# Rewriting the prologue of an induced attention block that feeds a gated feed-forward layer

## The chip, the cores and the metric

The kernel runs on one core of one Trainium2 chip. The metric is device time in microseconds (us) of one execution, lower is better, given as a median over runs. A profile is one execution taken by the hardware profiler; its span runs from the first to the last instruction and is a little shorter than the time. The engines are PE (matrix multiply, with its weight loads listed apart as PEld), DVE (vector), ACT (activation functions), POOL (GpSimd) and SP, which here only issues DMAs. POOL also issues DMAs. Each engine executes its own instructions in the order in which the program gives them.

## What is computed

Cut to what matters, with B = 4 batches of N = 12416 rows of C = 128 columns, m = 32 inducing rows, d_ff = 1536:

```python
def _attn_ref(x, inducing):
    scale = 1.0 / np.sqrt(C)
    I = np.broadcast_to(inducing[None], (B, m, C))
    def mab(q, kv):
        s = scale * (q @ kv.transpose(0, 2, 1))
        s = s - s.max(-1, keepdims=True)
        a = np.exp(s)
        a /= a.sum(-1, keepdims=True) + 1e-09
        return a @ kv
    h = mab(I, x)          # 32 rows per batch
    return mab(x, h)

def _moe_ref(x, w_gate, w_val, w_out):
    gate = 1.0 / (1.0 + np.exp(-(x @ w_gate)))
    return gate * (x @ w_val) @ w_out
```

All inputs and the output are float32; the kernel works in float16 with float32 sums.

## The kernel before

A batch of 12416 rows is 97 chunks of 128 rows. Chunks are taken in groups of 16 (`GC`): six full groups, numbered 0 to 5 (`NG` is 6), and a seventh of a single chunk, number `NG`. `groups` (before, the single chunk is chunk 96, the last one) gives the first chunk and the length of each group. `xn[b]` holds a batch of x with rows in partitions, `xT[b]` the same turned, so that columns lie in partitions.

The work of a batch has these parts.

- **Loads.** `x_load` (L76) issues one DMA on POOL's queue per group, which also casts to float16. All loads of batch 0, then the three weights `wg16`, `wv16`, `wo16` (L116 to L118), then all of batch 1 are issued at the start (L91 to L120). Later batches are loaded from within the main loop.
- **Stage 1**, the softmax over all 12416 rows for each of the 32 inducing rows. For a group: `x_turn` (L446) turns 16 chunks on PE and copies them out of PSUM, 8 by DVE (L453) and 8 by ACT (L454); `s1_score` gives scores (PE, L162) and their negated maximum `nm1` (DVE, L169); `s1_exp` (ACT, L181) gives exponentials and their sums `l1`; `s1_turn_pe` turns them on PE (L194) with a DVE copy (L196); `s1_sum` multiplies them with x (PE, L210) and ACT copies the result to `hst` (L217). The groups thus have a maximum of their own each.
- **Combine** (`combine`, from L250). The groups' maxima are brought to one: a DVE minimum over groups, a float32 matmul to bring 128 values into one row (L255), a minimum over the four partition groups (L257), a copy that spreads it (L261), a matmul back into a column (L266), a copy (L270). Then the groups' weights `w1` (ACT, L273), the weighted sums (L276 to L298), two float32 matmuls (L304, L305), the division (L307 to L311) that gives `hT`, and `hw`, which is h times the gate and value weights (L326 to L336). In batch 0 (`fast`) the weighted sum over groups is on DVE (L279, L284), in later batches on POOL.
- **Stage 2**, the softmax of each row over the 32 inducing rows: scores (L346), maximum (L357), which is split into two bfloat16 parts on POOL (L361, L363) and added on PE (L370), exponential (L379), sum, reciprocal (L405), the product spread to four copies (L407), and a turn by a DMA of SP's queue (`s2_turn_dma`, L417). The first four chunks (`BC`) of batch 0 are turned on PE instead (L485, L489).
- **Main loop.** A block of four chunks has 12 slices of d_ff in 8 steps. A step multiplies `a2` by `hw` for gate and value (PE, L535), takes tanh of the gate (ACT, L551), forms (t + 1) times the value (DVE, L560), and adds the product with `wo16` (PE, L590). A finished block is scaled by ACT (L597), turned by a DMA of SP (L599) and stored by a DMA of POOL (L608).

For batch 0, loads, stage 1, combine and the first group's stage 2 stand ahead of the main loop: this is the prologue. It is an order written out by hand (L459 to L492). Its loop transposes group i+2, scores group i+1, turns the exponentials of group i and sums group i-1 in one turn. Everything for the later batches is placed within the main loop by `beside`, by slots of two steps: `loads` and `work` hold the slot at which each begins; stage 1 of batch 1 begins at slot 5, and the DMA transposes of its x (`x_transpose_dma`, L85, on SP's queue) at slot 0.

PSUM is used up: the tags `g1`, `v1`, `m`, `acc` have one bank each, `g2` and `v2` two.

Of the kernel before, what the change touches and what calls it, by code (L numbers as in the profile page):

```python
# [16 lines left out]
P = 128  # L17
GC = 16
# [7 lines left out]
def kernel(  # L26
# [21 lines left out]
    groups = [(s * GC, GC) for s in range(NG)] + [(NG * GC, NLO)]  # L48
# [23 lines left out]
    def x_load(b, s):  # L72
        c0, n = groups[s]
        if b not in xn:
            xn[b] = xnp.tile([P, NCH, C], F16, tag="xn", name=f"xn_{b}")
        nc.gpsimd.dma_start(xn[b][:, c0 : c0 + n, :], xv[b, :, c0 : c0 + n, :])  # L76
# [37 lines left out]
    x_load(0, 5)  # L114
    x_load(0, 6)
    nc.gpsimd.dma_start(wg16[:], moe_w_gate.rearrange("c (i t f) -> c i t f", t=2, f=P))  # L116
    nc.gpsimd.dma_start(wv16[:], moe_w_val.rearrange("c (i t f) -> c i t f", t=2, f=P))
    nc.gpsimd.dma_start(wo16[:], moe_w_out.rearrange("(j p) c -> p j c", p=P))  # L118
    for g in range(len(groups)):
        x_load(1, g)  # L120
# [9 lines left out]
    one1 = const.tile([1, 1], F32, tag="one1")  # L130
    nc.vector.memset(one1[:], 1.0)
# [72 lines left out]
    def s1_sum(b, s, a1, tag):  # L204
# [12 lines left out]
        nc.scalar.copy(out=hsts[b % 2][0:R, s, :], in_=hp[0:R, :])  # L217
        summed[b] += 1

# [24 lines left out]
    def combine(b, fast):  # L244
        q = b % 2
        nm1, l1, hst = nm1s[q], l1s[q], hsts[q]
        while summed[b] < NS:
            yield
        mn = bp.tile([P, 1], F32, tag="mn")
        nc.vector.tensor_reduce(out=mn[:], in_=nm1[:], axis=AX.X, op=ALU.min)  # L250
        yield
        yield
        yield "take"
        row_ps = ps.tile([1, P], F32, tag="m", name="row_ps")
        nc.tensor.matmul(row_ps[:], mn[:], identf[:], start=True, stop=True)  # L255
        row = bp.tile([1, m], F32, tag="row")
        nc.vector.tensor_reduce(  # L257
            out=row[:], in_=row_ps[:].rearrange("o (g k) -> o k g", g=4), axis=AX.X, op=ALU.min
        )
        row4 = bp.tile([1, 4, m], F32, tag="row4")  # L260
        nc.vector.tensor_copy(out=row4[:], in_=row[:].unsqueeze(1).to_broadcast((1, 4, m)))  # L261
        yield "give"
        yield
        yield "take"
        col_ps = ps.tile([P, 1], F32, tag="m", name="col_ps")
        nc.tensor.matmul(  # L266
            col_ps[:], row4[:].rearrange("o g k -> o (g k)"), one1[:], start=True, stop=True
        )
        col = bp.tile([P, 1], F32, tag="col")
        nc.vector.tensor_copy(out=col[:], in_=col_ps[:])  # L270
        yield "give"
        w1 = bp.tile([P, NS], F32, tag="w1")
        nc.scalar.activation(out=w1[:], in_=nm1[:], func=AF.Exp, bias=col[:], scale=-1.0)  # L273
        yield
        lw = bp.tile([P, NS], F32, tag="lw")
        nc.vector.tensor_mul(out=lw[:], in0=l1[:], in1=w1[:])  # L276
        eng = nc.vector if fast else nc.gpsimd
        hx = bp.tile([P, NS, C], F32, tag="hx", bufs=1)
        eng.tensor_tensor(  # L279
            out=hx[:], in0=hst[:], in1=w1[:].unsqueeze(2).to_broadcast((P, NS, C)), op=ALU.mult  # L280
        )
        if fast:
            hsum = bp.tile([P, C], F32, tag="hsum")
            nc.vector.reduce_sum(out=hsum[:], in_=hx[:].rearrange("p s c -> p c s"), axis=AX.X)  # L284
            hsum = hsum[:]
        else:
            k = NS
            while k > 1:
                r = k // 2
# [28 lines left out]
        for hf in range(2):  # L318
            if not fast:
                yield "take"  # L320
# [16 lines left out]
            if not fast:  # L337
                yield "give"
# [391 lines left out]
```

## Time and profile before

| | |
|---|---|
| time, median of 3 runs | 794.26 us (793.11 to 795.95) |
| time of the profiled execution | 795.01 us |
| its span | 793.1 us |
| busy: PE, DVE, ACT, POOL | 670.7, 745.4, 672.8, 238.2 us |
| first matmul of the main loop | 38.75 us |
| first DVE product of the main loop (L560) | 40.45 us |
| last DVE product ends | 783.2 us |
| mean granted clock of PE | 0.967 |

Busy time is summed over the instructions of an engine. The three engines that compute are each busy for most of the span, DVE for 94% of it. A line of the timeline has the start in us, the length in us, the engine, the source line, the operation, written and read tiles, the shape, how many instructions are merged in it, and in brackets how long the engine was idle ahead of it and what ended that.

### The profile page before, as it was taken

Reading aid. Unit: us, or ns where it says so; the run is one execution under the profiler, and the core shown is the slowest. Engines: PE = TensorE matmul, PEld = TensorE weight load, DVE = VectorE, ACT = ScalarE, POOL = GpSimd, SP = SyncE. Lnnn points to the kernel's source line nnn. Section 1 sums busy time; section 2 is a strip of 40 time slices with the busy share of each in tenths; the row PEclk is TensorE's granted clock in tenths of the full one; section 3 lists DMA queues with packets and bytes.
Section 4 is the critical chain, followed back from the end, with each engine's and each line's share of the span. In section 5 each row is a group of like instructions: output and inputs, shape, how many; then the busy total and the mean of one; then the engine's idle time right before and its main releaser. Section 6 shows DMA issues by size and latency. Waiting matters only on the chain.

```text
span 793.1 us, 13966 instructions
## 1 busy us (share of the span) xinstructions
PE 670.7 (85%) x4729; PEld 230.8 (29%) x4729; DVE 745.4 (94%) x948; ACT 672.8 (85%) x1001; POOL 238.2 (30%) x396
## 2 busy tenths in 40 slices
PE   6588889888888888888888888988888888888884
PEld 4222223222232222322222222322323222223221
DVE  4689999999999999999998999999999999999994
ACT  4389989888989999878988898988898898899993
POOL 4131341532331422444404123143233133133200
PEclk9679999999999999989999999999999999999997
DMA  9958654536439566355338754241431431441421
GB/s 178 204 108 168 120 111 84 103 77 116 87 75 198 95 102 138 81 98 100 64 80 163 131 93 91 57 81 47 83 86 43 90 87 28 100 87 40 103 60 46
DMA packets 171015, 77.44 MB, mean 98 GB/s; under 512 B 154784, under 2 KB 155328, under 8 KB 170944
## 3 DMA queue, kind: packets, MB, share of 16 engines
q1 hardware_dynamic: 150672, 37.23, 28.8%
q0 software_dynamic: 20272, 39.33, 21.0%
q8 instruction: 37, 0.61, 0.3%
q14 instruction: 34, 0.28, 0.1%
HBM read 27.80 MB, written 25.43 MB: 67 GB/s over the span
## 4 chain that ended last, share of the span: by engine, by line
DVE 42%; PE 24%; issue 21%; ACT 10%; DMA 2%; POOL 0%; POOLq 0%; ACTq 0%; DVEq 0%
DVE u L560 37%; PE acc_ps L590 11%; PE v_ps L535 9%; ACT t L551 8%; DMA xn<-in_x_dram 2%; DVE nmx L357 2%; PE s_ps L370 1%; DVE nm L169 1%; PE g_ps L535 1%; ACT a1T L181 1%; ACT o L597 1%; DVE rs L405 1%; DVE hwt L336 0%; PE hp_ps L210 0%; PE s_ps L346 0%
## 5 line engine op out<-in xcount | busy, mean ns | idle before, releaser
L560 DVE SCALAR_TENSOR_TENSOR u<-t,v_ps 128x1024 f16<-128x1024 f16 (+1 forms) x776 | 693.1, 947 | 19.0 <-PE g_ps L535 7.3
L551 ACT ACTIVATE t<-g_ps 128x1024 f16<-128x1024 f32 (+1 forms) x776 | 598.8, 817 | 81.5 <-PE g_ps L535 67.0
L535 PE MATMUL v_ps<-a2r,hwt 32*128 32x512 f16 (+1 forms) x1188 | 294.7, 374 | 94.8 <-DVE u L560 87.6
L590 PE MATMUL acc_ps<-u,wo 128*128 128x512 f16 (+1 forms) x1200 | 325.2, 383 | 1.4 <-ACT o L597 0.7
L535 PE MATMUL g_ps<-a2r,hwt 32*128 32x512 f16 (+1 forms) x1188 | 297.4, 381 | 0.8 <-ACT t L551 0.6
L535 PEld LDWEIGHTS <-hwt 32*128 32x128 f16 x2400 | 102.8, 91 | 355.0 <-issue 346.7
L590 PEld LDWEIGHTS <-wo 128*128 128x128 f16 x1200 | 86.1, 98 | 145.3 <-issue 99.3
L407 POOL TENSOR_TENSOR a2n<-e,rs 128x2048 f16<-128x2048 f16 (+2 forms) x28 | 87.3, 3119 | 82.2 <-DVE rs L405 73.7
L608 POOL DMA_DIRECT2D out_dram<-on x100 | 57.0, 570 | 143.8 <-DMA on<-o 134.1
L597 ACT ACTIVATE o<-acc_ps 128x512 f16<-128x512 f32 (+1 forms) x100 | 59.2, 592 | 9.5 <-PE acc_ps L590 7.1
L361 POOL CAST hi<-nmx 128x16 bf16<-128x16 f32 (+3 forms) x29 | 5.7, 195 | 203.1 <-DVE nmx L357 203.0
L387 POOL TENSOR_TENSOR sum<-e 128x256 f32<-128x256 f16 (+1 forms) x27 | 16.0, 591 | 70.2 <-ACT e L379 70.2
L387 POOL TENSOR_TENSOR sum<-sum 128x128 f32<-128x128 f32 (+3 forms) x108 | 31.3, 290 | 8.5
L76 POOL DMA_DIRECT2D xn<-in_x_dram x28 | 15.4, 557 | 11.1 <-DMA xn<-in_x_dram 7.2
L346 PE MATMUL s_ps<-hT,xT 128*128 128x32 f16 x388 | 18.2, 180 | 0.6
L181 ACT ACTIVATE a1T<-s_ps,nm 128x512 f16<-128x512 f32 (+1 forms) x28 | 17.9, 639 | 0.4 <-DVE nm L169 0.4
L169 DVE TENSOR_REDUCE nm<-s_ps 128x1 f32<-128x512 f32 (+1 forms) x28 | 17.3, 618 | 0.5 <-PE s_ps L162 0.5
L346 PEld LDWEIGHTS <-xT 128*128 128x128 f16 x388 | 13.5, 97 | 13.4 <-issue 13.1
L357 DVE TENSOR_REDUCE nmx<-s_ps 128x16 f32<-128x512 f32 (+3 forms) x29 | 17.3, 596 | 0.0
L379 ACT ACTIVATE e<-s_ps 128x512 f16<-128x512 f32 (+3 forms) x29 | 15.2, 524 | 1.5 <-PE s_ps L370 1.5
L454 ACT COPY xT<-xt_ps 128x1024 f16<-128x1024 f16 x6 | 6.1, 1012 | 10.8 <-DVE xT L453 10.8
L453 DVE COPY xT<-xt_ps 128x1024 f16<-128x1024 f16 x6 | 4.1, 692 | 9.6 <-PE xt_ps L451 9.6
(78 smaller groups left out, 182.1 us busy)
## 6 DMA issues: line engine op xcount, KB each, us to landing
out_dram<-on POOLq DMA_DIRECT2D x96, 256.0 KB, 2.6
xn<-in_x_dram POOLq DMA_DIRECT2D x24, 512.0 KB, 8.5
on<-o SPq DMA_TRANSPOSE x100, 2.4
a2r<-a2n SPq DMA_TRANSPOSE x28, 6.0
wg<-in_moe_w_gate_dram POOLq DMA_DIRECT2D x1, 384.0 KB, 16.4
wv<-in_moe_w_val_dram POOLq DMA_DIRECT2D x1, 384.0 KB, 16.5
wo<-in_moe_w_out_dram POOLq DMA_DIRECT2D x1, 384.0 KB, 16.2
xT<-xn SPq DMA_TRANSPOSE x21, 4.7
```

The costliest lines, as they stand in the source:

```text
L169: nc.vector.tensor_reduce(out=nm1s[b % 2][0:R, s : s + 1], in_=s1[0:R, 0 : w * P], axis=AX.X, op=ALU.max, negate=True,)
L181: nc.scalar.activation(out=a1T[0:R, 0 : w * P], in_=s1[0:R, 0 : w * P], func=AF.Exp, bias=nm1s[b % 2][0:R, s : s + 1], accum_out=l1s[b % 2 ...
L346: nc.tensor.matmul(s2[:, j, :], xT[b][:, c + j, :], hT16[b][:], start=(j == 0), stop=False, skip_group_check=True,)
L357: nc.vector.tensor_reduce(out=nmx[:, 0:n], in_=s2[:, 0:n, :], axis=AX.X, op=ALU.max, negate=True)
L387: nc.gpsimd.tensor_tensor(out=d[:, 0:n, :], in0=src[:, :, 0:w], in1=src[:, :, w : 2 * w], op=ALU.add)
L407: eng.tensor_tensor(out=a2n[:, 0:n, :, :], in0=e[:, 0:n, :].unsqueeze(2).to_broadcast((P, n, 4, m)), in1=rs[:, 0:n].unsqueeze(2).unsqueeze ...
L535: nc.tensor.matmul(pt[:, k, col : col + W], hw[st["b"]][r : r + 32, j // 2, :], a2r[r : r + 32, o : o + nb, :].rearrange("p j t -> p (j t) ...
L551: nc.scalar.activation(out=st["t"][:, :, 0:w], in_=st["g"][:, :, 0:w], func=AF.Tanh, scale=0.5)
L560: nc.vector.scalar_tensor_tensor(out=st["u"][:, :, 0:w], in0=st["t"][:, :, 0:w], scalar=1.0, in1=st["v"][:, :, 0:w], op0=ALU.add, op1=ALU. ...
L590: nc.tensor.matmul(acc[:, 0:W], wo16[:, j, :], st["u"][:, k, col : col + W], start=first, stop=last)
L597: nc.scalar.mul(out=o16[:, 0:W], in_=acc[:, 0:W], mul=0.5)
L608: nc.gpsimd.dma_start(ov[st["b"], :, c : c + nb, :], on[:, 0:nb, :])
```

## The change

- The single chunk is now chunk 0 and the groups start at chunk 1. `x_load` of group 0 takes chunk 0 along (17 chunks, one DMA), and group 5 of batch 0 is loaded by two DMAs of 12 and 4 chunks. No load of x of the single chunk is left.
- Ahead of the prologue only x of batch 0 is loaded. `wg16` and `wv16` are issued on POOL behind the maximum of group 4, `wo16` and the first two loads of batch 1 behind the first group's stage 2 maximum, the other loads of batch 1 from within the main loop (slots 0, 3, 6, 9).
- The order of stage 1 in the prologue is a new one, shown below: the single chunk right behind group 0, then per group transposes, the turn of the group before, scores, exponentials, the sum of the group before. ACT now takes the first 8 chunks of `x_turn` and DVE the other 8, and neither waits for the other. The scores of group 4 stand ahead of group 5's transposes, its exponential behind them.
- The groups 0 to 2 and the single chunk get a common maximum of their own and are combined on POOL while groups 3 to 5 run. The weights of what is left are worked out from the maxima alone, by `s1_weights`, with copies from one group of 32 partitions to another in place of the two matmuls. The last group's sum is read from PSUM.
- `combine`, which is now for batches 1 to 3 only, uses `s1_weights` with all its copies and reductions on DVE.
- In the first stage 2, the maximum of the first four chunks is subtracted on DVE and doesn't go over POOL and PE; both copies of `hw` are on ACT; the remaining 12 chunks are spread as 4 on DVE and 8 on POOL, with a DMA transpose each.

The diff, cut to its core:

```diff
-    groups = [(s * GC, GC) for s in range(NG)] + [(NG * GC, NLO)]
+    groups = [(NLO + s * GC, GC) for s in range(NG)] + [(0, NLO)]
...
-    x_load(0, 5)
-    x_load(0, 6)
-    nc.gpsimd.dma_start(wg16[:], ...)
-    nc.gpsimd.dma_start(wv16[:], ...)
-    nc.gpsimd.dma_start(wo16[:], ...)
-    for g in range(len(groups)):
-        x_load(1, g)
+    x_load(0, 5, 12)
...
+    def s1_weights(nm1, eng):
+        n = nm1.shape[1]
+        quad = bp.tile([m, 4, n], F32, tag=f"quad{n}", name="quad")
+        for g in range(4):
+            eng.tensor_copy(out=quad[:, g, :], in_=nm1[32 * g : 32 * g + 32, :])
+        col = bp.tile([P, 1], F32, tag="col")
+        for g in range(4):
+            nc.vector.tensor_reduce(out=col[32 * g : 32 * g + 32, :],
+                in_=quad[:].rearrange("k g s -> k (g s)"), axis=AX.X, op=ALU.min)
+        w1 = bp.tile([P, n], F32, tag=f"w{n}", name="w1")
+        nc.scalar.activation(out=w1[:], in_=nm1, func=AF.Exp, bias=col[:], scale=-1.0)
+        return w1
+    def add_tree(eng, x, k):
+        while k > 1:
+            r = k // 2
+            eng.tensor_tensor(out=x[:, 0:r], in0=x[:, 0:r], in1=x[:, k - r : k], op=ALU.add)
+            k -= r
...
         if n == GC:
-            nc.vector.tensor_copy(out=xT[b][:, c0 : c0 + 8, :], in_=xt[:, 0, :, :])
-            nc.scalar.copy(out=xT[b][:, c0 + 8 : c0 + 16, :], in_=xt[:, 1, :, :])
+            one = nc.scalar.copy(out=xT[b][:, c0 : c0 + 8, :], in_=xt[:, 0, :, :])
+            for j0, j1 in ((8, cut), (cut, GC)) if cut else ((8, GC),):
+                two = nc.vector.tensor_copy(
+                    out=xT[b][:, c0 + j0 : c0 + j1, :], in_=xt[:, 1, j0 - 8 : j1 - 8, :])
+                tc.declare_no_dep(two.ins, one.ins, reason="each reads a bank of its own")
...
     x_turn(0, 0, "g2")
-    for i in range(-1, NS + 2):
-        if 0 <= i + 2 < NS:
-            x_turn(0, i + 2, ("g2", "v2")[i % 2])
-        if 0 <= i + 1 < NS:
-            aT_of[i + 1] = s1_exp(0, i + 1, s1_score(0, i + 1, ("g1", "v1")[(i + 1) % 2]))
-        if 0 <= i < NS:
-            a1_of[i] = s1_turn_pe(0, i, aT_of[i])
-        if 0 <= i - 1 < NS:
-            s1_sum(0, i - 1, a1_of[i - 1], "acc")
-    for _ in combine(0, True):
-        pass
+    x_turn(0, NG, "v2")
+    exp(0, score(0))
+    exp(NG, s1_score(0, NG, "v1"))
+    turn(NG)
+    total(NG)
+    last = NG - 1
+    for i in range(1, last):
+        x_turn(0, i, ("g2", "v2")[i % 2])
+        turn(i - 1)
+        s1 = score(i)
+        if i < last - 1:
+            exp(i, s1)
+        total(i - 1)
+        if i == early:
...
+            for k, s in enumerate(list(range(early)) + [NG]):
+                nc.gpsimd.tensor_scalar_mul(
+                    out=hx[:, k, :], in0=hst[:, s, :], scalar1=wf[:, k : k + 1])
+            hpart = add_tree(nc.gpsimd, hx, 1 + early)
+    x_turn(0, last, ("g2", "v2")[last % 2], 12)
+    exp(last - 1, s1)
+    exp(last, score(last))
+    nc.gpsimd.tensor_copy(out=nmf[:, 1:late], in_=nm1[:, early:last])
+    nc.gpsimd.dma_start(wg16[:], ...)
+    nc.gpsimd.dma_start(wv16[:], ...)
+    nc.gpsimd.tensor_copy(out=nmf[:, late:], in_=nm1[:, last:NG])
+    turn(last - 1)
+    total(last - 1)
+    w1 = s1_weights(nmf[:], nc.gpsimd)
+    turn(last)
+    hp = total(last, "g1", True)
...
+    nc.vector.tensor_scalar_mul(out=hsum[:], in0=hpart, scalar1=w1[:, 0:1])
+    for k in range(1, 1 + late):
+        nc.vector.scalar_tensor_tensor(out=hsum[:],
+            in0=hp[:] if k == late else hst[:, early + k - 1, :],
+            scalar=w1[:, k : k + 1], in1=hsum[:], op0=ALU.mult, op1=ALU.add)
...
+    s2_score(0, NLO, 0, BC, s2_a, True)
...
+    nc.vector.tensor_tensor(out=low[:], in0=s2_a[:, 0:BC, :],
+        in1=nmx_a[:].unsqueeze(2).to_broadcast((P, BC, m)), op=ALU.add)
...
+    hw_a = hw_fill(0, 0, "g1")
+    s2_score(0, NLO + BC, 0, GC - BC, s2_b)
     hl_b = s2_max(GC - BC, s2_b)
+    nc.gpsimd.dma_start(wo16[:], ...)
+    x_load(1, 0)
+    x_load(1, 1)
+    hw_b = hw_fill(0, 1, "v1")
...
+        if b == 0:
+            for g in range(2, NG):
+                loads.append((3 * (g - 2), "x", 1, g))
```

Here `score`, `exp`, `turn` and `total` are `s1_score`, `s1_exp`, `s1_turn_pe` and `s1_sum` for batch 0; `early` is 3 and `late` is 3; `hw_fill` issues the four matmuls of one half of `hw`.

## The prediction

> **What bounds the kernel now.** I read the page first. It puts 94% busy on DVE, and its costliest group is the gated product of the main loop:
>
> ```profile
> L560 DVE SCALAR_TENSOR_TENSOR u<-t,v_ps 128x1024 f16<-128x1024 f16 (+1 forms) x776 | 693.1, 947 | 19.0 <-PE g_ps L535 7.3
> ```
>
> So 693.1 of the 793.1 us of the span are one DVE instruction, repeated 776 times, with 19.0 us of idle time before it. The change leaves these 776 alone. What it can move is the stretch before the first of them, and whatever it adds to DVE between them. I therefore read the timeline of the first 45 us next (columns: start, length, engine, line, operation, tiles, count, and the idle time before it):
>
> ```profile
> 6.75 1.89 PE L451 MATMUL xt_ps<-ident,xn 128*128 128x128 f16 x16 [3.67 <-DMA xn<-in_x_dram]
> 8.68 0.69 DVE L453 COPY xT<-xt_ps 128x1024 f16<-128x1024 f16 x1 [4.95 <-PE xt_ps L451]
> 9.21 1.89 PE L451 MATMUL xt_ps<-ident,xn 128*128 128x128 f16 x16 [0.57 <-DMA xn<-in_x_dram]
> 9.40 1.01 ACT L454 COPY xT<-xt_ps 128x1024 f16<-128x1024 f16 x1 [7.40 <-DVE xT L453]
> 11.02 0.62 PE L162 MATMUL s_ps<-xT,indT 128*32 128x512 f16 x4
> 11.74 0.68 DVE L169 TENSOR_REDUCE nm<-s_ps 128x1 f32<-128x512 f32 x1
> 12.76 0.69 ACT L181 ACTIVATE a1T<-s_ps,nm 128x512 f16<-128x512 f32 x1
> 13.34 0.20 ACT L181 ACTIVATION_READ_ACCUMULATOR a1T<-s_ps,nm 128x1 f32 x1
> ...
> 19.05 1.07 PE L451 MATMUL xt_ps<-ident,xn 128*128 128x128 f16 x16 [0.28 <-DMA xn<-in_x_dram]
> ...
> 29.80 1.66 DVE L284 TENSOR_REDUCE hsum<-hx 128x128 f32<-128x896 f32 x1
> ...
> 38.75 0.61 PE L535 MATMUL g_ps<-a2first,hwt 32*128 32x512 f16 x2 [0.60 <-DVE a2first L489]
> ...
> 40.45 1.22 DVE L560 SCALAR_TENSOR_TENSOR u<-t,v_ps 128x1024 f16<-128x1024 f16 x1 [1.75 <-ACT t L551]
> ```
>
> Three things are to be seen. Loads of x land every 2.43 us (6.75, 9.2, 11.6 and so on to 19.05) and the PE transposes follow them: stage 1 of batch 0 keeps step with the loads. It can, because `x_turn` runs two groups ahead of the exponentials. From the last full group (19.05) to the first gate matmul (38.75) there pass 19.70 us, a chain with one instruction at a time. And the same 16 transposes take 1.89 us at first and 1.07 us later: PE starts at half its clock. It changes at 14.3 us, after 7.5 us of nearly unbroken work. After 24.8 it is at half again, and in the loop it works without a gap from 41.0 and is granted the full clock only at 48.7:
>
> ```profile
> 47.00:48.00 1.00, 1.00 (x6) 0.22 (x6) 0.53 (x1) 0.19 (x1) 0.00 (x0) 0.50 1.19 229
> 48.00:49.00 1.00, 1.00 (x4) 0.12 (x3) 0.93 (x1) 0.96 (x2) 0.00 (x0) 0.66 1.18 218
> 49.00:50.00 1.00, 1.00 (x9) 0.32 (x8) 0.98 (x2) 1.00 (x3) 0.37 (x1) 1.00 0.57 107
> ```
>
> (Busy time of PE, weight loads, DVE, ACT and POOL by microsecond; the third number from the end is the granted clock. Before 24 us this column shows 1.00 even where the transposes take 1.89, so there the durations speak.)
>
> **The change, part by part, against the profiled execution** (span 793.10, time 795.01, so 1.91 outside the span; the median is 794.26, 0.75 lower). I follow the first gate matmul, now at 38.75. Each hand-over between engines costs 0.05 in these rows.
>
> *Start of stage 1.* The first load has 17 chunks, 0.15 us more: transposes at 6.90 to 8.79. The two xT copies now run side by side, so the score waits for ACT's 1.01 alone (9.85) and not for 0.69 + 1.01: a gain of 0.7. Score 0.62, maximum 0.68, exponential 0.58: 11.85. Now the single chunk (group NG) is put ahead of group 1 on PE, and its exponential (0.35 + 0.18), transpose (0.18), copy (0.17) and sum (0.26) must follow group 0's on each engine. PE executes in order, so x_turn of group 1, whose data lie there at 9.35, starts at 13.0 and not 9.2. This costs 3.8.
>
> *The loop over groups 1 to 4.* The look-ahead is gone: ACT's queue reads copy(i), exp(i), hst(i-1), copy(i+1), and exp(i) needs the score that needs copy(i). At full clock one turn is copy 1.01, score 0.40, maximum 0.68, exponential until the next may start 0.58 + 0.10, hst 0.17, with hand-overs 3.09 us. At half clock PE closes the circle: transposes 1.89, copy 1.01, score 0.55, sum 0.50, hand-overs 0.10: 4.05 us. Both are longer than the 2.43 of the loads. The last group's transposes start at 13.04 + 4 x 4.05 = 29.2 at half clock, against 19.05 now: +10.2. At full clock after the first turn they start at 26.2: +7.1. That weights and the second batch's x are taken out of the queue ahead gains nothing here, since x was first in that queue already.
>
> *The last group to the gate.* The maxima are combined from nm alone, beside the sums: a POOL copy and four shifted copies (0.2 each, the nearest row is the 0.19 cast of 128x4, starts 0.12 apart), four DVE reductions (0.15 each by the 128x7 one), exponential 0.30. The two fp32 matmuls with their copies (25.2 to 28.2), the 1.08 multiply and the 1.66 reduction are off the path; in their place stand four 0.2 us multiply-adds. GpSimd's work on the early groups (eight small operations by 0.2; four scalings of 128x128, about 0.3; additions of 256 and 128 columns by the 0.72 and 0.45 of its add rows) is 4 us and ends by 29 to 30, before its result is wanted at 33 to 35: hidden; without cover it would cost those 4. The list from group 5's transposes: 1.89, copy 1.01, score 0.62, maximum 0.68, POOL 0.85, reductions 0.45, exponential 0.30, turn's copy 0.41, sum 0.62, multiply-add 0.22, h matmul behind the l matmul 1.1, hT 0.19, scores 0.35, maximum 0.29, subtraction 0.25, exponential 0.28 (both in DVE's shadow of the 0.54 maximum over the other 12 chunks, which stands ahead of the sum), sum to a2n 1.25, transposes 0.61, copy 0.36; with hand-overs 12.6. At full clock 10.9. So 19.7 becomes 12.6 or 10.9.
>
> *Weights.* wg and wv are issued on POOL behind group 4's maximum, at 29 to 32; load 0 took 2.4 us beyond its transfer to land, so they land about 6 us later for both, just ahead of their first use (35.8 at the earliest, 37.9 at half clock). wo is issued behind the casts of hi and lo (38 to 40) and wanted 4.9 us behind the gate. Priced at nothing; if they come late, PE stands for the difference, up to 1 us.
>
> *Sum of the prologue.* Half clock throughout: gate at 41.85, +3.1. Full clock from 21 us to 31: 39.7, +0.9. Full clock from 14.3 to the gate: 37.0, -1.7. The clock decides. In the new loop PE works 3.6 of 4.05 us with a gap in each turn; in the stretch 7.7 to 11.1 of now it worked 83% and was not lifted, and it took 7.5 and 7.7 us of almost gapless work the two times it was. I take +2.3, nearer the cold end. The Trainium skill speaks against that ("TensorE: Matmul & The Clock Gate", section "What's actually happening"): one busy window of some 3.4 us lifts the clock, so stage 1 would run at full speed from about 17 to 20 us and the prologue would come out at about +0.5. The 7.7 us above contradict that single window, so the sum does not use it.
>
> *The combine of batches 1 to 3*, in the loop where DVE has no idle time:
>
> ```profile
> 143.64 0.15 DVE L250 TENSOR_REDUCE mn<-nm 128x1 f32<-128x7 f32 x1
> 147.21 0.27 DVE L257 TENSOR_REDUCE row<-row_ps 1x32 f32<-1x128 f32 x1
> 147.51 0.21 DVE L261 COPY row<-row 1x128 f32<-1x128 f32 x1
> 151.14 0.15 DVE L270 COPY col<-col_ps 128x1 f32<-128x1 f32 x1
> ```
>
> These 0.78 us go. Four copies of 32x7 (between 0.06, the memset of 128x7, and 0.15, the copy of 128x1) and four reductions of 32x28 (between 0.15, of 128x7, and 0.28, of 32x128) come: 0.84 to 1.72. I take 0.15 + 0.15 four times, 1.2: +0.4 each, three times +1.2 (bounds +0.2 and +2.8). The skill ("VectorE: DVE Perf Modes", section "Two Vector instructions with no wait between them") says that an instruction that starts in another group of 32 partitions waits until all earlier ones have ended; the rows overlap by some 0.08 us, so eight such would add about 0.6 per combine.
>
> *The rest of the loop.* One small x load less per later batch: POOL idles here, nothing. Nothing else moves on DVE.
>
> Sum: +2.3 + 1.2 = +3.5. On the profiled execution 798.5, on the median 797.8; I give the latter.
>
> **The rivals.** *A, the clock comes early.* If the turns are dense enough, PE is at full clock from 14 to 17 us on; the gate comes at 37.0 (-1.7), and a clock still full at the loop's start saves up to 2 us more (eight steps took 9.9 us at half clock, 7.6 are normal). With the combine at its low bound: 794.26 - 3.5 + 0.2, about 791. For it: the 10.9 us tail; against: the tail's PE gaps. It decides if full clock holds from the second turn on. *B, a lift in the middle* (21 us): +0.9, with combine at +0.8, 796.0: no change that can be told. A measurement of this kernel tells 0.3%, 2.4 us, from nothing. *D, the second batch's x comes late.* It is issued only behind wo on POOL at 40 to 42, and SP's transposes of it (4.7 us) stand in the same queue as the output's. Estimated landing 46.5, transposed 51.2; PE meets its scores 13.2 us after the gate, at 55. With landing as slow as the 15.4 us that x loads took when queued, PE would stand 6.6 us, and DVE behind it. Half of that on top of the forecast: 801. For it: transposes and loads share full DMA engines at 43 to 49. Against: 3.9 us of slack. *The split last load does nothing* (copies wait for all 16 transposes, as at 8.68): in the sum already.
>
> **How the numbers follow.** Forecast 0.48 (796 to 799.5), A 0.19, B 0.20, D 0.13. Slower: D and all but 0.03 of the forecast, 0.58; same 0.23; faster 0.19. The range 791.5 to 800.8 leaves out half of A and most of D; the forecast's own is 796 to 799.5.
>
> **What would show it.** x_turn of group 1 behind the single chunk's sum, near 13 us; transposes in turns of 3 to 4 us and not 2.4; ACT idle before each exponential of stage 1; the last x_turn at 26 to 29; tail of 11 to 13; gate at 39 to 42; eight DVE operations per combine, 1.2 us together. I am wrong if the turns keep to 2.5 us, if the gate comes before 38, or if the loop from gate to end is shorter than 754.3 us.

## The result, and the profile after

The kernel after the change takes 807.68 us (median of 4 runs, 806.76 to 809.21), the kernel before, run beside it, 794.75 us (4 runs, 793.11 to 795.95). The ratio is 1.0166, 95% interval 1.0141 to 1.0191: 12.9 us slower. The forecast was slower too, but by 3.5 us, at 797.8.

The profiled execution after has a span of 805.0 us, 11.9 us longer than before. The costliest group of the page is the same product, and its busy time is unchanged (692.7 against 693.1 us), so what was added is waiting; the idle time right ahead of it went from 19.0 to 24.6 us:

```profile
L664 DVE SCALAR_TENSOR_TENSOR u<-t,v_ps 128x1024 f16<-128x1024 f16 (+1 forms) x776 | 692.7, 947 | 24.6 <-PE g_ps L639 7.6
```

Because the 776 products are the same ones in the same order, the start of the k-th product after, less its start before, says where the time went:

```
product     0      6      7      8     20     40    100    115    140    480    760    775
lag, us  +2.56  +2.11  +8.90  +9.62  +9.62  +9.62  +9.97  +14.5  +11.4  +10.6  +10.6 +11.59
```

Three pieces are to be seen: 2.6 us from the prologue, 7.1 us more by product 8 (a stride of 7.5 between the products 6 and 8, as the lag had first come down to 2.11), and about 2 us in the rest, with a rise of 4.5 us near product 115 that is partly given back. First the prologue, in the timeline of PE after the change:

```profile
6.58 2.00 PE L453 MATMUL xt_ps<-ident,xn 128*128 128x128 f16 x17 [3.44 <-DMA xn<-in_x_dram]
...
12.59 0.29 PE L206 MATMUL hp_ps<-xn,a 128*32 128x128 f16 x1 [0.27 <-DVE a L192]
12.81 1.89 PE L453 MATMUL xt_ps<-ident,xn 128*128 128x128 f16 x16
...
16.78 1.89 PE L453 MATMUL xt_ps<-ident,xn 128*128 128x128 f16 x16
...
20.33 1.07 PE L453 MATMUL xt_ps<-ident,xn 128*128 128x128 f16 x16
...
26.72 1.07 PE L453 MATMUL xt_ps<-ident,xn 128*128 128x128 f16 x16
...
41.31 0.61 PE L639 MATMUL g_ps<-a2first,hwt 32*128 32x512 f16 x2 [0.52 <-DVE a2first L591]
...
49.68 0.39 PE L639 MATMUL v_ps<-a2first,hwt 32*128 32x512 f16 x2
55.98 0.60 PE L639 MATMUL g_ps<-a2r,hwt 32*128 32x512 f16 x2 [5.91 <-DMA a2r<-a2n]
```

Group 1's transposes start at 12.81, behind the single chunk's sum (12.59), and the next follow after 3.97, 3.55, 3.07 and 3.32 us instead of 2.43. The last group starts at 26.72, 7.7 us later than before; the way from there to the first gate matmul is 14.59 us instead of 19.70. That leaves +2.56 at the gate (41.31 against 38.75).

The last line is the big piece. PE wants the second block's `a2r`, and stands 5.91 us for a DMA. Before, the same matmuls had no wait (47.36, below). SP's queue shows which DMA it is after the change (columns: start, time until the queue was past it, issue, tiles, count):

```profile
47.36 0.61 PE L535 MATMUL g_ps<-a2r,hwt 32*128 32x512 f16 x2
...
42.94 9.45 SPq L419 DMA_TRANSPOSE a2r<-a2n  x2
52.43 6.25 SPq L89 DMA_TRANSPOSE xT<-xn  x2
```

The transpose of the second four chunks (tile `a2second`, which carries the name a2r) is issued at 42.94 and is there when PE goes on, at 55.98: 13.0 us. DVE waits behind PE (its next product starts at 58.19, after 6.79 us without work). The granted clock goes down with it; these are windows of 2 us, with the clock, the DMA share and GB/s at the end of each line:

```profile
50.00:52.00 2.00, 0.07 (x2) 0.00 (x0) 1.31 (x2) 0.00 (x0) 0.00 (x0) 1.00 1.06 209
52.00:54.00 2.00, 0.00 (x0) 0.00 (x0) 0.00 (x0) 0.00 (x0) 0.00 (x0) 0.70 1.09 215
54.00:56.00 2.00, 0.02 (x2) 0.02 (x2) 0.00 (x0) 0.00 (x0) 0.00 (x0) 0.50 1.12 204
```

From 52 to 56 us hardly any engine works, and the DMA engines are full. Their packets by queue, first from 43 to 56 us, then from 47 to 54 us, then from 56.5 to 59 us (q0 is POOL's queue, q1 is SP's; packets, MB, share):

```profile
q0 software_dynamic: 1404, 2.34, 97.0%
q1 hardware_dynamic: 1539, 0.39, 18.1%
...
q0 software_dynamic: 372, 1.38, 97.5%
q1 hardware_dynamic: 369, 0.09, 9.8%
...
q1 hardware_dynamic: 2613, 0.66, 123.5%
```

While POOL's loads of `wo16` and of x of batch 1 run, SP's transposes get 1539 packets in 13 us, 118 per us. Once the loads are through they get 2613 in 2.5 us, 1045 per us: nine times as many. Where x loads alone stand against them, from 47 to 54 us, the two queues move nearly the same number of packets (372 and 369), but 1.38 MB against 0.09. In the kernel before no load was in flight there, and its one transpose of 12 chunks landed in 4.0 us (the last number), unnoticed:

```profile
a2r<-a2n SPq DMA_TRANSPOSE x1, 4.0
```

### The profile page after: what moved, and what is told of

Same layout as the page of the kernel before. It is cut to its first block, busy times and chain, and to the rows that moved or that the text cites. A ratio compares the mean times of both kernels' runs of the same rounds, so it can differ in the third digit from the quotient of the medians.

```text
span 805.0 us, 13957 instructions
## 1 busy us (share of the span) xinstructions
PE 671.0 (83%) x4711; PEld 230.3 (29%) x4711; DVE 746.4 (93%) x963; ACT 672.8 (84%) x1002; POOL 242.8 (30%) x413
## 4 chain that ended last, share of the span: by engine, by line
DVE 43%; issue 22%; PE 21%; ACT 10%; DMA 3%; POOL 1%; POOLq 0%; DVEq 0%; ACTq 0%
DVE u L664 38%; PE acc_ps L694 9%; PE v_ps L639 7%; ACT t L655 7%; DVE nmx L352 2%; DMA a2r<-a2n 2%; PE s_ps L365 1%; DVE nm L165 1%; PE g_ps L639 1%; ACT a1T L177 1%; DVE rs L403 1%; ACT o L701 1%; PE xt_ps L453 1%; DMA xn<-in_x_dram 1%; ACT xT L455 0%
## 5 line engine op out<-in xcount | busy, mean ns | idle before, releaser
L664 DVE SCALAR_TENSOR_TENSOR u<-t,v_ps 128x1024 f16<-128x1024 f16 (+1 forms) x776 | 692.7, 947 | 24.6 <-PE g_ps L639 7.6
L356 POOL CAST hi<-nmx 128x16 bf16<-128x16 f32 (+2 forms) x28 | 5.5, 196 | 206.5 <-DVE nmx L352 206.5
L352 DVE TENSOR_REDUCE nmx<-s_ps 128x16 f32<-128x512 f32 (+2 forms) x28 | 17.0, 606 | 0.6 <-PE s_ps L341 0.6
L374 ACT ACTIVATE e<-s_ps 128x512 f16<-128x512 f32 (+2 forms) x28 | 14.9, 532 | 0.8 <-PE s_ps L365 0.8
L158 PE MATMUL s_ps<-xT,indT 128*32 128x512 f16 (+1 forms) x100 | 10.8, 400 | 5.2 <-ACT xT L455 5.1
```

The source lines that it names most:

```text
L352: nc.vector.tensor_reduce(out=nmx[:, 0:n], in_=s2[:, 0:n, :], axis=AX.X, op=ALU.max, negate=True)
L664: nc.vector.scalar_tensor_tensor(out=st["u"][:, :, 0:w], in0=st["t"][:, :, 0:w], scalar=1.0, in1=st["v"][:, :, 0:w], op0=ALU.add, op1=ALU. ...
```

## The experiments

All times are medians beside runs of the kernel before on the same chip (its medians there: 793.80 to 794.82 us). Theory: most of the loss is that collision, so it is the place of the loads, not the new prologue, that costs; what is left is the lost look-ahead. Rivals: the first x of batch 1 is late (rival D), the new combine, the half clock.

| kernel | time, us | ratio to before, 95% interval |
|---|---|---|
| e1_loads_ahead | 798.21 | 1.0049, 1.0031 to 1.0067 |
| e2_x_later | 819.69 | 1.0333, 1.0277 to 1.0389 |
| e3_old_combine | 806.81 | 1.0163, 1.0129 to 1.0198 |
| e4_chunk_later | 805.03 | 1.0132, 1.0107 to 1.0158 |
| e5_lookahead | 797.38 | 1.0029, 1.0008 to 1.0050 |
| e6_look_old_combine | 796.60 | 1.0030, 1.0011 to 1.0049 |
| e7_warm_pe | 800.48 | 1.0079, 1.0048 to 1.0110 |
| e8_before_loads_late | 804.12 | 1.0117, 1.0083 to 1.0152 |
| e9_full_skew | 795.73 | 1.0018, 1.0000 to 1.0036 |
| e10_full_skew_new_combine | 795.92 | 1.0016, 1.0004 to 1.0028 |
| e11_two_groups_early | 791.33 | 0.9963, 0.9946 to 0.9981 |

**The loads back in front (e1).** The changed kernel with the weights and all of batch 1's x issued right behind batch 0's x:

```diff
     x_load(0, 5, 12)
+    nc.gpsimd.dma_start(wg16[:], ...)
+    nc.gpsimd.dma_start(wv16[:], ...)
+    nc.gpsimd.dma_start(wo16[:], ...)
+    for g in range(NG):
+        x_load(1, g)
...
-    nc.gpsimd.dma_start(wg16[:], ...)
-    nc.gpsimd.dma_start(wv16[:], ...)
...
-    nc.gpsimd.dma_start(wo16[:], ...)
-    x_load(1, 0)
-    x_load(1, 1)
...
-        if b == 0:
-            for g in range(2, NG):
-                loads.append((3 * (g - 2), "x", 1, g))
```

> The changed kernel with the three weights and all of batch 1's x issued right behind batch 0's x, as before; nothing else differs. Theory (the DMA transpose of chunks 4 to 7, tile a2second, lands 13 us after its issue because wo and batch 1's x fill the 16 DMA engines): those loads are over by 40 us, the transpose lands in 4 to 5 us, the 5.9 us wait of PE for it near 50 us is gone, gate still at 41.3, span about 798 and time about 800.5 (7 us less than the change). Rival 1 (the transpose is late because its DVE product is 1.6 us later than before's, or because it is now two transposes): the wait stays at 4 us or more and the time at 806 to 808. Rival 2 (the deferred loads helped the prologue): the gate comes later than 41.3.

798.21 us: 9.5 us of the 12.9 are gone. In its timeline, PE and SP in turn:

```profile
48.50 0.39 PE L639 MATMUL g_ps<-a2r,hwt 32*128 32x512 f16 x2
...
41.88 2.99 SPq L424 DMA_TRANSPOSE a2r<-a2n  x2
```

The same two transposes are past SP's queue in 2.99 us instead of 9.45, the first `a2r` matmul has no wait, and the lag at product 8 is +0.55. The first product also comes 1.05 us earlier (41.96 against 43.01), so the loads in their new place did not help the prologue either.

**The loads alone, on the kernel before (e8).** Nothing of the new prologue, only `wo16` and batch 1's x moved to where the change puts them:

```diff
-    nc.gpsimd.dma_start(wo16[:], ...)
-    for g in range(len(groups)):
-        x_load(1, g)
...
+    nc.gpsimd.dma_start(wo16[:], ...)
+    x_load(1, 0)
+    x_load(1, 1)
     e_a = s2_exp(BC, s2_a, *hl_a)
...
+        if b == 0:
+            for g in range(2, NS):
+                loads.append((3 * (g - 2), "x", 1, g))
```

> The kernel before with one part of the change alone: wo and batch 1's x are issued where the change issues them (wo and two groups behind the first stage 2 maxima, the rest from slots 0, 3, 6 and on). Theory (the loads in the loop hold up the DMA transpose that the second block waits for): the a2r transpose issued at 41.3 lands after 50, PE waits 3 to 7 us for it near 47, and the time is 798 to 803. Rival (it was the split into two transposes, or the later DVE product): no wait over 1 us, time within 1.5 us of before.

804.12 us, some 9.4 above the kernel before and a little more than expected. Its timeline has the same wait (PE), and its DMA issues from 41 to 55 us the same landing (the last number). Here it is one transpose and not two, so the split is not the cause:

```profile
54.63 0.61 PE L535 MATMUL g_ps<-a2r,hwt 32*128 32x512 f16 x2 [6.93 <-DMA a2r<-a2n]
...
a2r<-a2n SPq DMA_TRANSPOSE x1, 13.5
```

One part of the change, put alone on the old kernel, thus makes its largest loss; taken out of the new kernel (in e1 together with the two gate weights), it takes that loss away. That is shown from both sides.

**Which loads, and whether later is better (e2).** `wo16` stays, batch 1's x is loaded from slot 5 on, and batch 1's stage 1 begins 12 slots later:

```diff
-    x_load(1, 0)
-    x_load(1, 1)
...
-            for g in range(2, NG):
-                loads.append((3 * (g - 2), "x", 1, g))
+            for g in range(NG):
+                loads.append((5 + 3 * g, "x", 1, g))
...
-                loads.append((at + 3 * g, "t", b + 1, g))
+                loads.append((at + late_by(b) + 3 * g, "t", b + 1, g))
```

(`late_by` is 12 for batch 0 and 0 otherwise; the slots of stage 1 and combine move with it.)

> The changed kernel with batch 1's x issued from slot 5 of the main loop on, one group each three slots, and its DMA transposes and stage 1 put 12 slots later; wo stays where the change has it. If x of batch 1 is what delays the a2second transpose, it lands within 6 us, no wait near 50 us, time 800 to 801. If wo alone, or the transpose itself, is to blame, the wait stays at 3 us or more and the time at 804 to 808. If the later stage 1 of batch 1 runs into a wait of its own, the lag against before grows between products 20 and 100.

The wait at 50 us is gone: the lag is +1.16 at product 20. But the kernel is the slowest of all, 819.69 and not 800 to 801. The loads now meet other transposes. PE stands for two of them, and SP's queue, in which they all stand, shows why:

```profile
78.62 0.61 PE L637 MATMUL g_ps<-a2r,hwt 32*128 32x512 f16 x2 [6.38 <-DMA a2r<-a2n]
109.98 0.62 PE L206 MATMUL hp_ps<-xn,a 128*32 128x128 f16 x16 [6.12 <-DMA a<-a1T]
...
60.90 6.51 SPq L419 DMA_TRANSPOSE a2r<-a2n  x1
67.45 3.16 SPq L701 DMA_TRANSPOSE on<-o  x1
70.66 10.79 SPq L89 DMA_TRANSPOSE xT<-xn  x1
```

The `a2r` that PE wants at 72 is issued at 60.90 and lands only at 78.6. The second transpose (`a`) lands within 2.8 us of its issue, but is issued only at 107.17, behind others in the queue, though its input was ready at 101.8. The lag is +16.8 by product 60 and +21 and more later. So the loss is no matter of one unlucky tile: x loads that stay in flight cost whichever transpose is wanted next. A short meeting costs nothing: in e5 and e11 below, x loads are also in flight when block two's transposes are issued, until 45.6 and 41.1 us, but the transposes land within 3.5 and 4.5 us and PE has no wait for them. `wo16` is not to blame. From 43 to 47 us in this kernel it moves 795 packets beside the transposes' 1458, and these land in 2.8 us:

```profile
q0 software_dynamic: 795, 0.20, 50.4%
q1 hardware_dynamic: 1458, 0.37, 46.2%
a2r<-a2n SPq DMA_TRANSPOSE x2, 2.8
```

Those packets are of 256 bytes (0.20 MB in 795), while the loads of x bring packets of 4096 bytes, which took 322 ns each in e8 (median) against 18 ns for one of a transpose. The Trainium skill ("DMA: Bandwidth & Descriptors", section "SWDGE vs HWDGE vs iDMA") says that a DMA engine takes its queues in turn and switches at packets. The 372 and 369 packets above agree with turns of one packet: then small ones lose little to small ones and much to large ones. No run here varies the size of packets alone, so the size as the reason stays an explanation.

**The combine (e3).** The function `combine` of the kernel before in batches 1 to 3, all else as changed:

```diff
-            work.append((at + 5 + 6 * NS, 1, lambda b=b: combine(b + 1)))
+            work.append((at + 5 + 6 * NS, 1, lambda b=b: combine(b + 1, False)))
```

> The changed kernel with the earlier combine (two float32 matmuls and five small DVE operations) for batches 1 to 3. If the eight small DVE operations of the new combine cost what the prediction says, the loop gets 0.4 us per combine shorter, 1.2 us in all, time 806.5. If they cost nothing, as DVE would have waited anyway, 807.7. If the lag that builds up near product 120 (4 us, of which 2 are given back) is the new combine's, it is gone and the loop is 1.5 to 2 us shorter.

806.81, 0.87 us less than with the new one, inside the spread of either (803.63 to 808.97 here), so the times don't tell whether the new combine costs anything. The trace does: the lag near product 120, +13.6 in the changed kernel, is +9.6 here. The rise near there is the new combine's; more on it behind the experiments. Two more pairs follow below.

**The single chunk one turn later (e4).** Its second transpose and sum moved behind group 1's transposes:

```diff
-    turn(NG)
-    total(NG)
...
         x_turn(0, i, ("g2", "v2")[i % 2])
+        if i == 1:
+            turn(NG)
+            total(NG)
         turn(i - 1)
```

> The changed kernel with the turn and the sum of the single chunk moved behind the 16 transposes of group 1 on PE. Theory (those two, in order on PE, hold group 1 back from 9.2 to 12.8 us): group 1's transposes start at 9.2 to 9.4, ACT copies them once its two exponentials are out (12.1 and not 14.7), and the gate comes 2.6 us earlier, near 38.7; the time falls by 2 to 3 us, to 805, as the wait for a2second follows it. Rival (the clock or the loads set the start of the turns): the gate moves by less than 1 us.

Group 1's transposes start at 10.27 and not 9.2 (they now stand behind the scores of 9.64), and the first product comes 1.25 us earlier, half of what was expected: the turns after it are 4.64, 3.97, 3.54 and 3.32 us, since PE's transposes turn fast only after 21.5 us. The time is 805.03, 2.65 less; in the profiled executions the lag at the last product is 1.0 less. That the time is the one expected proves little, as the gate moved only half as far; the wait for the second block (5.79) is as long as before. The single chunk in front is a cost, of 1 to 2.7 us.

**Half a look-ahead (e5).** Group i+1 is transposed ahead of group i's scores, and loads are mostly early (weights and three of batch 1's groups in front, three behind POOL's last work of the prologue):

```diff
-    for i in range(1, last):
-        x_turn(0, i, ("g2", "v2")[i % 2])
-        turn(i - 1)
+    x_turn(0, 1, "v2")
+    for i in range(1, NG):
+        if i < last:
+            x_turn(0, i + 1, ("v2", "g2")[i % 2], 12 if i + 1 == last else 0)
         s1 = score(i)
...
+        turn(i - 1)
+        exp(i, s1)
+        if i < last:
+            total(i - 1)
```

> The changed kernel with three things undone: x_turn runs one group ahead of the scores again, the single chunk's turn and sum stand behind group 2's transposes, and weights and batch 1's x are issued early (three groups at the start, three behind the last POOL work of the prologue). The short tail (all maxima and sums as in the change) is kept. Theory (the change lost its gain of 7 us in the tail to the missing look-ahead and to loads put into the loop): group 5's transposes at 19.2 to 19.5, the gate 12.4 to 13.5 us later at 32 to 33, no wait near block 2, time 788 to 791, 4 to 6 us less than before. Rival 1 (GpSimd's work on the early groups, 4.8 us in the changed kernel's trace, is no longer hidden when the groups come faster): gate at 34 to 36, time 791 to 793. Rival 2 (the a2second transpose, issued at 35, still meets the loads, which end near 40): a wait of 2 us or more near 42.

A miss: 797.38 us, and the first product is at 42.90, no earlier than in the changed kernel (and 0.94 later than in e1). The wait for `a2r` is gone, as expected. Its timeline of PE:

```profile
20.09 0.61 PE L196 MATMUL aT_ps<-ident,a1T 128*128 128x128 f16 x4
21.32 0.62 PE L212 MATMUL hp_ps<-xn,a 128*32 128x128 f16 x16 [0.63 <-DVE a L198]
21.87 1.89 PE L459 MATMUL xt_ps<-ident,xn 128*128 128x128 f16 x16
```

The sum (L212) follows the second transposes of the same group (L196) and waits for DVE's copy of them; the next x transposes stand behind it in PE's order. Such a wait in every turn makes 4.15 us of it, at the slow length of 1.89 up to the last group at 26.03. The kernel before sums a group one turn later than it turns it, so this wait is covered.

**The combine again (e6).** e5 with the old combine, by the same edit as in e3:

```diff
-            work.append((at + 5 + 6 * NS, 1, lambda b=b: combine(b + 1)))
+            work.append((at + 5 + 6 * NS, 1, lambda b=b: combine(b + 1, False)))
```

> The kernel of e5 with the earlier combine for batches 1 to 3. Measured in the changed kernel's trace, the new combine has 1.69 us of DVE copies and reductions where the earlier one has 0.78: 0.9 us more each, 2.7 us in all. Theory: 1 to 3 us less than e5. Rival (DVE's extra operations fall into time that other engines cost anyway): the same time within 0.5 us.

796.60 against 797.38: 0.8 us less, between the two expectations, and the intervals of the two ratios overlap almost wholly.

**Clearing the clock by empty work (e7).** e1 with twelve matmuls on a tile of zeros ahead of all else:

```diff
+    warm = const.tile([P, 512], F16, tag="warm")
+    nc.vector.memset(warm[:], 0.0)
+    for _ in range(12):
+        warm_ps = ps.tile([P, 512], F32, tag="acc", name="warm_ps")
+        nc.tensor.matmul(warm_ps[:], warm[:, 0:P], warm[:], start=True, stop=True)
```

> The kernel of e1 (loads ahead) with twelve 128x512 matmuls on zeros put on PE while it waits for the first x, from about 1.2 to 6.4 us; they feed nothing. Theory (at half clock a turn of stage 1 takes 4.0 us and at full clock 3.1; the clock is lifted by work without gaps): if the clock is lifted by 7 us, group 1's transposes take 1.07 and not 1.89, the turns take 3.1 from the first one on, the last x_turn starts near 24 and the gate comes 1.5 to 2.5 us earlier than in e1; time 796. Rival (the turns are not bound by the clock): the gate moves by less than 0.5 us. If 5 us of such work do not lift the clock, the first 16 transposes still take 1.89 and nothing changes.

800.48, 2.3 us more than e1, and the first product comes 2.3 us later (44.22). The timeline of PE:

```profile
1.18 7.65 PE L100 MATMUL warm_ps<-warm 128*128 128x512 f16 x12 [1.18 <-DVE warm L97]
8.76 0.63 PE L151 MATMUL indT_ps<-identf,ind 32*128 32x32 f32 x2
9.32 1.99 PE L463 MATMUL xt_ps<-ident,xn 128*128 128x128 f16 x17
```

They held PE to 8.83, past the landing of x, and the 17 transposes behind them still took 1.99 us, as when PE had done nothing. Their length, and that of the x transposes up to those that start at 19.53 (1.89), is that of the half clock. This kernel says nothing on what an early clock would be worth, as it never had one.

**The whole look-ahead (e9), and with the new combine (e10).** The prologue's loop in the skew of the kernel before, with the single chunk among the first two groups, on top of e6 (the loop that it takes the place of is left out here):

```diff
+    x_turn(0, 1, "v2")
+    x_turn(0, NG, "m")
     exp(0, score(0))
...
+    for i in range(0, NG - 1):
+        if i + 2 < NG:
+            x_turn(0, i + 2, ("g2", "v2")[i % 2], 12 if i + 2 == last else 0)
+        exp(i + 1, score(i + 1))
+        if i == 0:
+            exp(NG, s1_score(0, NG, "acc"))
+        turn(i)
+        if i == 1:
+            turn(NG)
+        if i > 0:
+            total(i - 1)
+        if i == 2:
+            total(NG)
```

> e6_look_old_combine with the loop of the prologue in the skew that the kernel before has: while the transposes of group i run, the scores of group i-1, the second transposes of group i-2 and the sum of group i-3 are issued, the single chunk among the first two groups; the combine early on GpSimd, the short tail, the old combine for batches 1 to 3 and the early loads stay. Theory (what the prologue lost is its look-ahead: in the change a turn of the loop waits in full for its own copies): the x transposes follow one another by about 2.5 to 3.2 us as in the kernel before, the last group starts at about 19 to 21 us and not at 26 to 27, the first product comes at 34 to 37 us instead of 42.9, and the time is 789 to 792. Rival (the half clock sets the turns, whatever the order): the turns stay near 4 us until the clock rises, the last group starts after 24 us, and the time stays at 795 to 798.

> e9_full_skew with the combine of the change in batches 1 to 3. Theory (this combine holds VectorE 0.9 us longer in each batch, where PE waits for VectorE in the loop): 0.5 to 2.5 us above e9_full_skew. Rival (VectorE's slack in the loop takes it): within 0.4 us of it.

Half right. The last group's transposes start at 21.05 instead of 26.00 in e6, in 1.07 us. The first two turns take 2.44 and 2.47 us though the transposes in them still take 1.89 and 1.99, so the order does that and not the clock; from about 13 us on the clock is fast as well, which e6 has only from 29 us on, so the 5.0 us belong to both together. But the first product comes only 1.8 us earlier (41.02), and the time, 795.73, is not the theory's. The 3 us are lost on GpSimd. Lines of e9 on PE, DVE and POOL:

```profile
32.03 0.62 PE L214 MATMUL hp_ps<-xn,a 128*32 128x128 f16 x16 [5.38 <-DVE a L200]
...
30.84 0.68 DVE L257 TENSOR_REDUCE col<-quad 32x1 f32<-32x16 f32 x4 [5.54 <-POOL quad L254]
...
28.41 1.25 POOL L283 TENSOR_TENSOR hx<-hx 128x256 f32<-128x256 f32 x2
29.60 0.19 POOL L599 COPY nmf<-nm 128x2 f32<-128x2 f32 x1
```

PE waits 5.38 us for a DVE copy; that copy stands behind DVE's reductions; these wait for POOL's copies of the maxima; and those stand behind the early combine (to 29.60), though the last maximum was there at 24.8. e10 is 0.2 us above e9, as its rival had it. With e3 and e6, the medians put the new combine at 0.2 to 0.9 us in all, and none of the three differences is clear of zero.

**Less on GpSimd (e11).** Two groups in the early combine instead of three, and the last group's turn and sum ahead of the reductions:

```diff
-    early = NG - 3
+    early = NG - 4
...
-    w1 = s1_weights(nmf[:], nc.gpsimd)
     turn(last)
     hp = total(last, "g1", True)
+    w1 = s1_weights(nmf[:], nc.gpsimd)
```

> e9_full_skew with two groups and the single chunk, not three and the chunk, in GpSimd's early combine, and with the last group's second transposes and sum ahead of the weights' reductions on VectorE. In e9_full_skew VectorE's reductions wait until 30.84 us for copies that stand on GpSimd behind the early combine (24.82 to 29.60), and PE waits 5.4 us for VectorE behind them. Theory (this queue on GpSimd holds the end of the prologue): the early combine is over by about 26, the four reductions end near 28, the first product comes 2.5 to 3.5 us earlier than in e9_full_skew (at 37.5 to 38.5), and the time is 791.5 to 793.5. Rival (something else holds the end, as PE's or ACT's own work): the first product within 0.8 us of e9_full_skew's 41.0, the time 795 to 796.5.

791.33 us, ratio 0.9963 (0.9946 to 0.9981): 3.05 us faster than the kernel before, which had 794.38 beside it. POOL and PE of e11:

```profile
24.59 0.99 POOL L283 TENSOR_TENSOR hx<-hx 128x128 f32<-128x128 f32 x2
25.52 0.19 POOL L599 COPY nmf<-nm 128x3 f32<-128x3 f32 x1
...
26.68 0.41 PE L214 MATMUL hp_ps<-xn,a 128*32 128x128 f16 x16 [0.52 <-DVE a L200]
29.80 0.64 PE L623 MATMUL l_ps<-e,lb 128*128 128x32 f32 x2 [2.71 <-POOL lb L277]
```

The maxima's copies start 4.1 us earlier, PE's wait ahead of the sum falls from 5.38 to 0.52, and the first product is at 37.35: 3.1 us ahead of the kernel before, and still 3.7 ahead at product 100. Two things were changed at once here; their shares were not measured apart.

## Why the prediction was right and wrong

**The start of stage 1 was right.** x_turn of group 1 was put at 13.0 and came at 12.81. The price of that, 3.8 us, was too high as a cost of the end: e4 gave back 1.25 us at the first product.

**The loop's turns were right.** "The look-ahead is gone" foresaw 3.09 us at full clock and 4.05 at half; measured 3.97 at the slow length, 3.07 and 3.32 at the fast one. The last group was to start at 26.2 to 29.2 (the terms given add up to 26.4 at the fast end) and did at 26.72. e9 shows what the look-ahead is worth, together with the clock.

**The clock was no rule.** The sum leaned to the cold end because it had taken 7.5 and 7.7 us of almost gapless work to lift the clock. Those were two readings of one execution: in e8, whose PE instructions up to there are those of the kernel before, its matmuls are fast from 10.9 us on, 4.3 us after the first transposes, and in the changed kernel they are fast again 3.6 us after the long wait (55.98, 59.6).

**The tail was right in its links and too short in size.** 12.6 or 10.9 us were foreseen, 14.59 came. GpSimd's scalings of 128x128 took 0.59 us each and not 0.3, so that the early combine ended at 30.12, just as the last maximum came (30.08), and no longer ahead of it. Behind it stood what the step on the weights, "Priced at nothing", left out. It looked at when they land, not at their issue on POOL in the middle of that chain:

```profile
30.07 0.19 POOL L526 COPY nmf<-nm 128x2 f32<-128x2 f32 x1
30.20 0.64 POOL L527 DMA_DIRECT2D wg<-in_moe_w_gate_dram  x1
30.82 0.55 POOL L528 DMA_DIRECT2D wv<-in_moe_w_val_dram  x1
31.35 0.22 POOL L529 COPY nmf<-nm 128x1 f32<-128x1 f32 x1
31.63 0.83 POOL L246 COPY quad<-nmf 32x4 f32<-32x4 f32 x4
```

The two issues hold the last maximum's copy 1.2 us (30.20 to 31.35). And `wv16` landed 6.4 us after its issue, at 37.2, which held PE's first matmul with it some 0.4 us behind that with `wg16` (37.27 and 36.91; in e1 they start at 36.21 and 36.20). e1, which has neither, has a tail of 13.08 us. What is left lies in several links: the four multiply-adds took 1.38 us and not 0.8, and DVE's sum over the first four chunks starts 0.7 us behind its input (38.72, 37.98), as the maximum over the other 12 stands ahead of it. That the prologue came out near what was said, +2.56 for +2.3, is in part luck: the loop was nearer its fast end and the tail longer than either forecast.

**The combine's DVE time was too low, and a part of its price was missed.** Foreseen was +0.4 us of DVE each and +1.2 us in the time. Lines of DVE and PE around 154 us, and the 2 us from 160 us on (the clock is the third number from the end):

```profile
153.61 0.96 DVE L246 COPY quad<-nm 32x7 f32<-32x7 f32 x4
154.61 0.73 DVE L249 TENSOR_REDUCE col<-quad 32x1 f32<-32x28 f32 x4
...
156.11 0.37 PE L639 MATMUL v_ps<-a2r,hwt 32*128 32x512 f16 x1 [1.96 <-DVE u L664]
...
160.00:162.00 2.00, 1.68 (x9) 0.38 (x4) 2.00 (x3) 1.51 (x2) 0.47 (x1) 0.50 1.13 178
```

1.69 us, for 0.78 that went: +0.9 each, within the bounds given (0.84 to 1.72 in place of 0.78), at their upper end. The copies start 0.24 us apart and the reductions 0.18, more than the 0.15 assumed; the rule of held instructions cited there, with some 0.6 us per combine, would have come nearer. These eight stand in one piece: PE waits 1.96 us behind them, and its clock, 1.00 until then, is down to 0.50 from 160 to 164 us. In e3, with the old combine, it stays at 1.00 there. The lag rises from 9.97 at product 103 to 14.5 at product 115 and is back at 11.4 by product 136. In all the kernels here, a rise of about 4 us goes with the new combine (e2's comes later, as its stage 1 does), and none with the old one. Why most of it is given back was not followed. What remains is not settled: from product 100 to the end the lag of the profiled executions grows by 2.9, 2.1 and -0.1 us more with the new combine (e3, e6, e9 against their pairs), and the medians differ by 0.87, 0.78 and 0.19. The +1.2 in time is neither shown nor refuted.

**The step that failed is what the change does to the DMA transposes.** The text followed the moved loads to their own landing ("if they come late, PE stands for the difference, up to 1 us") and, in rival D, to the transposes of batch 1's x, and asked whether PE would miss those at 55 us. It wrote that "transposes and loads share full DMA engines at 43 to 49" (before the change, SP's transposes alone fill them then, with 4997 packets and none of POOL's queue), and drew no price for the transposes that were already there: that of the second block of `a2` appears in no term of the sum, "the rest of the loop" was put at nothing, and the transposes of x were taken at 4.7 us. That transpose is issued at 42.94 and wanted at 50.07, 7.1 us later; at the 4.0 us that twelve chunks took before it would have been hidden, at 13.0 it is late by the 5.9 us seen, and with the restart at half clock it cost 7.1. D had the right cause, with a chance of 0.13, but watched another victim. That one was late too: its load landed at 47.4 (46.5 was estimated), its transpose only at 58.5 and not at 51.2, and PE was to meet those scores 13.2 us behind the gate, at 54.5. It cost nothing because PE already stood for `a2r` until 55.98 and met them at 61.60, without a wait: the lag stays at 9.62 us from product 8 to 40. Without the collision the time comes to what was forecast, but by luck in part: e1, 798.21, is 3.4 us above the kernel before, for a sum of +3.5, yet in its profiled execution +0.55 of that is there by product 8 (for +2.3) and +2.9 comes behind it (for +1.2).

**What stays open.** Turns of one packet are not the whole of it: in e8 the DMA engines are busy for only 0.34 of the time from 50 to 52 us, while the transpose and a load are both under way, and in e2 the transposes of 71 to 78 us get 1226 packets in 7 us beside only 36 of the loads. The remaining +2 us between product 8 and the end were followed only as far as the combine.

## What to carry to other kernels

A load that is moved is to be priced twice: for when it lands, and for every transfer that is in flight while it runs, above all the small ones that something waits for. Its issue is an instruction as well, and belongs to the chain of the engine that makes it. And work put on an idle engine to take it off the path stands ahead of whatever that engine must do next: here the early combine on GpSimd paid only once it was short enough that the last maximum waits 1.2 us for its copies (24.3 to 25.5 in e11) and not 4.8 (24.8 to 29.6 in e9).

## What the runs showed of the hardware

- The DMA transposes of four and of eight chunks land in 2.9 us (median of the two, e1) with no load in flight; the one of four took 13.0 us beside loads of x. One of twelve chunks took 4.0 and 13.5 (before and e8). SP's queue is held meanwhile: two issues took 2.99 and 9.45 us.
- How long PE works at half clock before it is fast was not one number: 7.5 us in the kernel before, 4.3 us in e8 with the same PE instructions up to there, 3.6 us behind the wait in the changed kernel. In e7, 7.65 us of gapless matmuls on zeros did not do it, nor did the 1.99 us of transposes that followed. The Trainium skill ("TensorE: Matmul & The Clock Gate", section "What's actually happening") has one busy window of about 3.4 us suffice; the 3.6 and 4.3 us agree with that, the 7.5 us and e7 don't. Whether it is the zeros that make the difference was not tried with other data.
- While x loads and DMA transposes were both in flight without a pause (47 to 54 us of the changed kernel), they moved 372 and 369 packets.
- GpSimd took 0.59 us for a float32 scaling of 128x128 by a column, and 0.64 and 0.55 us to issue the loads of `wg16` and `wv16` (1.09 for `wo16`).
